# A gated mix of an S5 scan and an H3 long convolution: ssm_D put into the kernel's first column by ScalarE, and two orders of TensorE's work changed

## The chip, the cores and the metric

The kernel runs on one core of a Trainium2 chip. The metric is the time of one execution on the device, in microseconds (us), lower being better. The time before is 382.72 us, the median of three runs (378.66, 382.72 and 385.46). A further execution was profiled. In the text TensorE is PE (PEld its weight loads), VectorE DVE, ScalarE ACT, GpSimd POOL and SyncE SP, as in the profile.

## What is computed

Two layers over the same x (2048 x 1024, bf16) are mixed by a gate for each row. One is a diagonal state-space layer with complex states (S5); the other, H3, shifts k with a kernel of four taps, multiplies by v, convolves every channel causally with a kernel as long as the sequence, adds the input times ssm_D, and multiplies by q, which here is x.

```python
g = sigmoid((x * gate_w).sum(-1, keepdims=True))
Bu = einsum("bld,pd->blp", x, B_bar)            # B_bar complex
h[t] = Lam_bar * h[t - 1] + Bu[t]
a = 2 * einsum("blp,dp->bld", h, Cmat).real + x * Dskip
k_shift = sum over t of k_pad[:, t:t + S] * shift_k[:, ks - 1 - t]
kv = k_shift * v
y = irfft(rfft(kv, 2 * S) * rfft(ssm_k, 2 * S))[:S]
y = y + kv * ssm_D
b = x * y
out = g * a + (1 - g) * b
```

Adding kv * ssm_D after a convolution is the same as adding ssm_D to the first tap of the convolution's kernel, ssm_k[:, 0]. Both kernels do it in that way.

## The kernel before, in words

**Stages.** The 1024 channels of H3 are done in eight groups of 128, numbered 0 to 7; loop c of `for c in range(NC - 1)` (line 1190) works on several groups at once, as a software pipeline: the products of group c, the spectra of group n = c + 1, the folds and taps of group nn = c + 2, and the inverse of group c - 1. Beside them TensorE does the first S5 products ("B's half tiles": tiles `odd` and `even` of Bu, the generator `parts`, line 1187). After the loops come the rest of S5: products with B (tile `both`), scans on VectorE, products with C (tile `psy`), the mix and the stores.

**One group of H3.** The sequence is cut into four blocks of 512, and a transform of the block is computed by matmuls with tables of cosines and sines (CF, SF, NCF forward; CI, SI back). Ahead of the forward transform a block is folded into its even and odd parts about the middle.

- `fold_columns` (line 506) folds ssm_k's group (tile kn, channels on partitions) for groups 0 and 2 to 6. Its first step writes the reversed first half `lo` (`back`), on ScalarE for all groups but 0. Its second and third step each fill one PSUM tile `foldk` by eight matmuls against the identity, four from kn and four from lo, and ScalarE copies it into `eok`, half mt = 0 and half mt = 1. In the tile mt = 1, two more matmuls with one row of weights (`withD`, lines 522 to 526) add ssm_D, read from the row sD (sD is the first partition of `rows_`). Groups 1 and 7 are folded by `fold_K` and `mirror_K`, which add ssm_D by a matmul too.
- `fwd_K(n, fis)` (line 636) makes K's spectrum, one PSUM tile `psk` for each of four values of fi, eight matmuls each (four for group 7). The first matmul of a tile reads half 0 of eok, the second half 1. ScalarE copies psk into one of two buffers, in the trace BT.
- `taps` and `times_v` (lines 573 and 603) make k_shift * v; `times_v` has a product on VectorE, then two matmuls into `mirror`, which ScalarE copies as `lo`, then VectorE's `ev`, and a gather, an adding DMA issued by POOL, ks<-lo.
- `fwd_V` (line 674) makes v's spectrum (`psv`), from ev and ks; ScalarE copies it into Vh.
- `products` (line 687) multiplies the spectra on VectorE, ending with two writes to Vh.
- `inverse` (line 769) reads Vh by 16 matmuls into two tiles `psz`; ScalarE copies each into cv, and SP stores it to cv_scr in DRAM.

**What sets the order.** Every engine's instructions are written in a fixed order: `put` (line 93) chains each to the one before on its engine, so the order of the calls in the loop is the order on each engine. Each step waits on its engine until its operands are there. All PSUM tiles come from one pool of four (line 82): a tile takes the place of the fourth before it and waits until that one is copied out. The pool for eok has one buffer, that for lo two. DMAs are issued by SP in the order of the calls; an issue that waits holds up all behind it. `hold` (line 182) has ScalarE write one column of a tile, so that a load into it waits for ScalarE.

**The loop around the change (lines 1233 to 1322), from c = 1.** The order is: the inverse of c - 1, the mirror of times_v, four steps of products, the rest of times_v, the matrices of taps (`dgs`), the first step of fold_columns, `fwd_K` for fi 0 and 1, then 2 and 3, the rest of fold_columns, half tiles, taps, loads, the rest of products, `fwd_V` for fi 0 and 1, half tiles, `fwd_V` for fi 2 and 3. In loop 0 (lines 1192 to 1226) the rest of fold_columns(2) follows fwd_V (`run(fk)`, line 1216) and is TensorE's last work in that loop. In loop 5 the last two half tiles follow `fwd_V(6)`.

Of the kernel before, what the change touches and what calls it, by code (L numbers as in the profile page):

```python
# [10 lines left out]
ACT = mybir.ActivationFunctionType  # L11
BF16 = mybir.dt.bfloat16
F32 = mybir.dt.float32
# [7 lines left out]
def kernel(  # L21
# [76 lines left out]
    def mm(o, l, r, first, last):  # L98
        put("pe", nc.tensor.matmul, o, lhsT=l, rhs=r, start=first, stop=last)
# [15 lines left out]
    def copy(o, a):  # L115
        put("dve", V.tensor_copy, o, a)

    def act(o, i, **kw):
        put("act", nc.scalar.activation, out=o, in_=i, **kw)
# [34 lines left out]
    sD = rows_[0:1]  # L154
    skr = rows_[32:32 + ND, 0:128 * KS].rearrange("j (p k) -> j p k", k=KS)
    gwr = rows_[32:32 + ND, 128 * KS:128 * KS + 128]
    prow = rows_[64:64 + 3 * ND, 0:128]

    nc.scalar.dma_start(out=skr, in_=B_shift_k.rearrange("(j p) k -> j p k", p=128))
# [159 lines left out]
    copy(fr_, fr_i)  # L319
    pcol = consts.tile([128, 3 + KS, ND], F32, name="pcol")  # L320
    gwb = consts.tile([128, ND], BF16, name="gwb")
    pcol2 = consts.tile([128, 4, ND], F32, name="pcol2")
    ident2 = consts.tile([128, 64], BF16, name="ident2")
    psp = ps2([128, 2, 512], "p")
# [12 lines left out]
    def columns():  # L337
        mm(psp[:, 0, 0:3 * ND], prow, ident[64:64 + 3 * ND, 64:64 + 3 * ND], True, True)
        copy(pcol[:, 0:3], psp[:, 0, 0:3 * ND].rearrange("p (i j) -> p i j", j=ND))
        yield  # L340
        psp2 = ps2([128, 2, 512], "p")
        mm(psp2[:, 1, KS * ND:(KS + 1) * ND], gwr, ident[32:32 + ND, 32:32 + ND], True, True)
        for q in range(4):
            for t in range(2):
                mm(psp2[t * 64:t * 64 + 64, 1, 64 + q * ND:64 + (q + 1) * ND],
                   skr[:, q // 2 * 64:q // 2 * 64 + 64, q % 2 + 2 * t], ident[32:32 + ND, 32:32 + ND], True, True)
        yield
        copy(gwb, psp2[:, 1, KS * ND:(KS + 1) * ND])
        copy(pcol2, psp2[:, 1, 64:64 + 4 * ND].rearrange("p (i j) -> p i j", j=ND))
        tt(ident2, ident[:, 0:64], ident[:, 64:128], ALU.add)  # L350

# [154 lines left out]
    def fold_columns(c):  # L506

        kn = lds.pop(("kn", c)).rearrange("p (a t) -> p a t", t=TB)
        back = eo_pool.tile([128, 4, 2, 128], BF16, name="lo", bufs=2)
        rev = back.rearrange("p a f d -> p a (f d)"), kn[:, :, 255::-1]  # L510
        if c == 0:
            copy(*rev)
        else:
            act(*rev, func=ACT.Copy)
        yield
        eo = eos["k", c] = eo_pool.tile([128, 2, 2, 4, 128], BF16, name="eok")
        for mt in range(2):
            ps = ps2([128, 4, 2, 128], "foldk")
            for a in range(4):
                mm(ps[:, a], kn[:, a, 256 + mt * 128:384 + mt * 128], idents[:, 0:2], a % 2 == 0, False)  # L520
            for a in range(4):
                withD = mt == 1 and a == 0
                mm(ps[:, a], back[:, a, mt], idents[:, 1:3], False, a % 2 == 1)
                for e in range(2 if withD else 0):

                    mm(ps[:, a, e], refl[0:1, e], sD[:, c * 128:(c + 1) * 128], False, False)
            act(eo[:, :, mt], ps.rearrange("p a e d -> p e a d"), func=ACT.Copy)
            yield
# [123 lines left out]
    def first_K():  # L652

        eo, KH[0] = eos["k", 0], spectrum("K", 0)
        pss = [ps2([128, 2, 4, 128], "psk") for fi in range(2)]
        for mt in range(2):
            for fi, ps in enumerate(pss):
                fsl = slice(fi * 128, (fi + 1) * 128)
                for cc in range(2):
                    mm(ps[:, cc], (CF, SF)[cc][:, mt, fsl], eo[:, cc, mt], mt == 0, False)  # L660
                    mm(ps[:, cc, 1:4], (SF, NCF)[cc][:, mt, fsl], eo[:, 1 - cc, mt, 0:3], False, mt == 1)
                if mt == 1 and fi == 0:
                    act(of_tile(KH[0], fi), ps, func=ACT.Copy)
                elif mt == 1:
                    copy(of_tile(KH[0], fi), ps)
# [455 lines left out]
    def step(gen):  # L1121
        next(gen, None)

    def run(gen):
        for _ in gen:
            pass
# [32 lines left out]
    load("kT", 1)  # L1159
    load("v", 1)  # L1160
    load("kn", 1)
    first_K()
    run(angles)
    fwd_V(0, (0, 1))
# [25 lines left out]
    for c in range(NC - 1):  # L1190
        n, nn = c + 1, c + 2
        if c == 0:
            load("kn", 2)
            load("kT", 2)
            load("v", 2)
            load_BT(0, 0)
            load_xT(0, (1,))
            p1 = products(0, 1)
            fwd_K(n, (0, 1))
            steps(p0, 2)  # L1200
            run(tv)
            dg = dgs(nn, True)
            steps(p1, 2)
            step(p0)
            step(p1)
            run(p0)
            taps(nn, dg)
            step(sp)
            fk = fold_columns(nn)
            step(fk)  # L1210
            fwd_K(n, (2, 3))
            step(p1)
            step(sp)
            fwd_V(n)
            run(p1)
            run(fk)
            tv = times_v(nn)
            step(tv)
            load("kn", 3)
            load("kT", 3)  # L1220
            load_BT(0, 1)
            apart = spread(3)
            step(apart)
            load_xT(0, (0,))
            run(apart)
            continue
        if c == 6:
            put("pool", nc.gpsimd.tensor_copy, stamp, xTs[2][:, 0, 0:HB + 1:HB])
        if c == 6:
            CT[1] = ct_pool.tile([128, 2, D], BF16, name="CT1")  # L1230
            load_CT(1)
            move(rows_, bc(A_Dskip.rearrange("(o d) -> o d", o=1), [128, D]))
        tabs, back, prod = turn_table(c - 1) if c <= NG else none, inverse(c - 1), products(c)
        step(old)
        step(tabs)
        if c == 6:
            step(parts)
        run(back)
        step(tv)
        steps(prod, 4)  # L1240
        run(tv)
        step(old)
        step(tabs)
        run(old)
        fk = none
        if nn < NC:
            dg = dgs(nn)
            if by_channel(nn):
                fk = fold_columns(nn)
                step(fk)  # L1250
        if c == 2:
            step(parts)
        fwd_K(n, (0, 1))
        if c in (2, 6):
            step(parts)
        fwd_K(n, (2, 3))
        if c == 1:
            lam_diag(0, lam_pool, True)
        if c == 4:
            step(parts)  # L1260
        if c == 6:
            run(sp)
            s5p["Q"] = s5p["wu"]
            run(turns_U[2])
            gate(0)
        step(prod)
        if nn < NC:
            if not by_channel(nn):
                fk = mirror_K(nn)
            step(fk)  # L1270
            if c < 5:
                step(fk)
            if c == 4:
                step(parts)
            if c == 1:
                load_BT(1, 0, True)
            elif c in (2, 4):
                load("v", nn, True)
            step(parts)
            taps(nn, dg)  # L1280
            if c == 5:
                load("v", nn)
                load_xT(2, held=True)
            if nn + 1 < NC:
                load("kT", nn + 1, True)
                load("kn", nn + 1)
                apart = spread(nn + 1)
                step(apart)
                if c == 1:
                    load_BT(1, 1)  # L1290
                elif c in (2, 3):
                    load_xT(1, (3 - c,))
                run(apart)
        step(prod)
        run(fk)
        run(prod)
        if n == NC - 1:
            overlap_K(n)
        if nn < NC:
            tv = times_v(nn)  # L1300
            step(tv)
            step(parts)
        else:
            run(next(tiles))
            CT[0] = ld.tile([128, 2, D], BF16, name="CTa", tag="ld")
            hold(CT[0][:, 0, 0:1])
            load_CT(0)
            load_BT(2, 0)
            load_BT(2, 1)
            run(next(tiles))  # L1310
            run(next(tiles))
        fwd_V(n, (0, 1))
        if c < 6 and c != 4:
            step(parts)
            if c in (1, 3):
                step(parts)
        fwd_V(n, (2, 3))
        if c in (4, 5):
            step(parts)
        if c == 1:  # L1320
            lam_diag(1, lam_pool)
        old = tabs
# [291 lines left out]
```

## Time and profile before

| | |
|---|---|
| median of three runs | 382.72 us (378.66 to 385.46) |
| the profiled execution | 379.12 us, its span 377.3 us |
| granted TensorE clock | 1.00 |
| busy, of 377.3 us: PE, DVE, ACT, POOL | 370.3, 367.8, 303.9, 76.3 us |
| the chain that ended last: PE, issue, DMA | 90%, 5%, 3% |
| HBM read and written | 16.01 and 8.39 MB |

The profile is one execution. Its rows come from several views: the page; groups of instructions; the waits (engine, what it was about to write, whom it waited for: total us, times, longest us); the chain of waits, which goes back from the last instruction to whatever released it; windows (length, busy us of PE, PEld, DVE, ACT and POOL with the number of instructions, the granted clock, the share of the DMA engines, GB/s); and the timeline (start, length in us, engine, line, operation, written tile <- read tiles, shape, count). Nearly every instruction has line 95, that of `put`, so rows are told apart by their tiles. A row with a count groups successive instructions: its length runs from the first's start to the last's end. A matmul's row is longer than its share of the engine, because matmuls overlap: the distance between starts, the pitch, is what one costs.

### The profile page before, as it was taken

The numbers are of one execution on the slowest core, as the hardware profiler recorded it, in microseconds if no ns is written. First come the engines' busy times: TensorE is split into PE (matmuls) and PEld (weight loads), VectorE is DVE, ScalarE is ACT, GpSimd is POOL, SyncE is SP. The second block draws the span as 40 slices with busy tenths as digits, with TensorE's granted clock in tenths as the row PEclk, the third lists the DMA queues.
The fourth block names the chain that finished last, engine by engine and source line by source line (L and its number), as shares of the span: only waits on it lengthen the run. The fifth ranks groups of instructions, "written<-read, shape, count | busy, mean of one in ns | idle before, by whom it ended". The sixth has DMA issues, their size and how long they took to land.

```text
span 377.3 us, 6661 instructions
## 1 busy us (share of the span) xinstructions
PE 370.3 (98%) x2442; PEld 201.8 (53%) x2477; DVE 367.8 (97%) x596; ACT 303.9 (81%) x465; POOL 76.3 (20%) x106
## 2 busy tenths in 40 slices
PE   8999999999999999999999999999999999999996
PEld 5657567575674847644454444444444444444444
DVE  8999999999999999999999999999999999999975
ACT  5979998988979999687999699978879967946301
POOL 4011030120301203022012013122425323532000
PEclk9999999999999999999999999999999999999999
DMA  7889999999989879998999999746999998996223
GB/s 169 169 141 244 222 219 202 234 217 223 222 188 214 166 167 197 195 202 145 222 210 236 225 197 241 165 75 117 193 240 159 270 247 180 193 248 119 57 83 112
DMA packets 121827, 70.99 MB, mean 188 GB/s; under 512 B 98425, under 2 KB 103425, under 8 KB 121794
## 3 DMA queue, kind: packets, MB, share of 16 engines
q1 hardware_dynamic: 108416, 45.90, 54.6%
q0 software_dynamic: 12256, 24.38, 37.4%
q10 hardware_dynamic: 1122, 0.28, 0.4%
q8 instruction: 19, 0.31, 0.3%
q14 instruction: 14, 0.11, 0.1%
HBM read 16.01 MB, written 8.39 MB: 65 GB/s over the span
## 4 chain that ended last, share of the span: by engine, by line
PE 90%; issue 5%; DMA 3%; SPq 0%; POOL 0%; ACT 0%; DVE 0%; POOLq 0%; ACTq 0%
PE psy L95 29%; PE both L95 22%; PE psk L95 11%; PE psz L95 6%; PE psv L95 6%; PE taps L95 4%; PE foldk L95 4%; PE even L95 3%; PE odd L95 3%; DMA ks<-lo 2%; DMA kT<-in_B_k_dram 1%; PE p L95 1%; PE mirror L95 1%; SPq L95 0%; POOL acc L95 0%
## 5 line engine op out<-in xcount | busy, mean ns | idle before, releaser
L95 PE MATMUL psy<-CT,U 128*128 128x512 bf16 (+1 forms) x418 | 92.7, 374 | 0.4
L95 PEld LDWEIGHTS <-U 128*128 128x128 bf16 x492 | 48.1, 98 | 55.6 <-issue 0.3
L95 PEld LDWEIGHTS <-BT 128*128 128x128 bf16 x544 | 50.5, 98 | 33.5 <-issue 0.2
L95 DVE TENSOR_TENSOR wkh<-BT,Vh 128x2048 bf16<-128x2048 bf16 (+3 forms) x31 | 44.6, 1458 | 0.0
L95 POOL DMA_DIRECT2D U<-Q x26 | 26.6, 1035 | 80.6 <-ACT Q L95 33.0
L95 DVE TENSOR_TENSOR acc<-BT,Vh 128x4096 bf16<-128x4096 bf16 (+3 forms) x19 | 36.9, 1948 | 0.3 <-ACT Vh L95 0.2
L95 ACT ACTIVATE Q<-U,lam 128x512 bf16<-128x512 bf16 (+1 forms) x60 | 35.0, 626 | 1.4 <-issue 1.3
L95 PE MATMUL both<-xT,BT 128*128 128x512 bf16 x157 | 35.2, 379 | 0.2
L95 ACT ACTIVATE Vh<-psv 128x1024 bf16<-128x1024 f32 x32 | 30.6, 1033 | 5.6 <-PE psv L95 5.5
L95 DVE TENSOR_TENSOR_SCAN A<-rv,init,A 128x256 bf16<-128x256 f32 x48 | 34.4, 736 | 0.0
L95 DVE TENSOR_TENSOR acc<-acc,wkh 128x1024 bf16<-128x1024 bf16 (+4 forms) x30 | 32.7, 1128 | 0.1
L95 ACT ACTIVATE BT<-psk 128x1024 bf16<-128x1024 f32 x31 | 30.1, 1046 | 2.3 <-PE psk L95 2.2
L95 ACT ACTIVATE U<-both 128x512 bf16<-128x512 f32 x44 | 24.3, 594 | 8.1 <-PE both L95 7.8
L95 POOL DMA_DIRECT2D acc<-wkh x8 | 9.7, 1218 | 100.7 <-DVE wkh L95 100.7
L95 PEld LDWEIGHTS <-SF 128*128 128x128 bf16 x184 | 18.0, 98 | 19.6 <-issue 0.9
L95 PE MATMUL psk<-eok,SF 128*128 128x384 bf16 (+1 forms) x118 | 28.0, 354 | 0.2
L95 ACT ACTIVATE BT<-psy,gcols 128x1024 bf16<-128x1024 f32 (+1 forms) x6 | 6.3, 1043 | 25.6 <-issue 14.6
L95 PE MATMUL psz<-Vh,CI 128*128 128x512 bf16 x64 | 24.3, 379 | 0.0
L95 PE MATMUL psz<-Vh,SI 128*128 128x512 bf16 x64 | 24.3, 379 | 0.0
L95 PEld LDWEIGHTS <-kT 128*128 128x128 bf16 x352 | 21.5, 101 | 1.6 <-DMA kT<-in_B_k_dram 1.1
L95 PE MATMUL taps<-dg,kT 128*128 128x128 bf16 (+1 forms) x352 | 22.1, 212 | 0.1
L95 DVE TENSOR_TENSOR U<-U,trn 128x512 bf16<-128x512 bf16 (+1 forms) x60 | 22.0, 390 | 0.1
(225 smaller groups left out, 780.1 us busy)
## 6 DMA issues: line engine op xcount, KB each, us to landing
U<-Q POOLq DMA_DIRECT2D x26, 256.0 KB, 4.7
acc<-wkh POOLq DMA_DIRECT2D x6, 768.0 KB, 8.1
cv_scr<-cv SPq DMA_DIRECT2D x16, 256.0 KB, 3.6
kn<-in_B_ssm_k_dram SPq DMA_DIRECT2D x6, 512.0 KB, 3.9
v<-in_B_v_dram SPq DMA_DIRECT2D x2, 1024.0 KB, 6.9
out_dram<-m SPq DMA_DIRECT2D x8, 256.0 KB, 4.2
BT<-cv_scr SPq DMA_DIRECT2D x7, 256.0 KB, 6.0
out_dram<-BT SPq DMA_DIRECT2D x7, 256.0 KB, 2.0
```

The source lines that it names most:

```text
L95: i = f(*a, **kw)
```

## The change

Three things are changed.

1. ssm_D for groups 2 to 6. ssm_D is loaded a second time, as eight rows of 128 (drow, a part of `rows_`), by an issue on SP behind the loads of group 1. One matmul against the identity turns it into columns, and ScalarE copies them to `dcol`. In fold_columns ScalarE then adds a group's column to kn's first column, in place, ahead of the reversing copy; the matmuls of `withD` remain for group 0 alone.
2. K's spectrum. From loop 1 on, `fwd_K` for fi 0 and 1 stands in front of the inverse; fi 2 and 3 stay where they were. In loop 6 all four stand in front.
3. B's half tiles. At the end of loop 5 all that is left of `parts` runs in front of `fwd_V(6)`, v's sixth spectrum.

```diff
@@ -154,6 +154,7 @@
     gwr = rows_[32:32 + ND, 128 * KS:128 * KS + 128]
+    drow = rows_[32:32 + ND, 128 * KS + 128:128 * KS + 256]
@@ -319,6 +320,7 @@
     gwb = consts.tile([128, ND], BF16, name="gwb")
+    dcol = consts.tile([128, ND], F32, name="dcol")
@@ -340,12 +342,14 @@
         mm(psp2[:, 1, KS * ND:(KS + 1) * ND], gwr, ident[32:32 + ND, 32:32 + ND], True, True)
+        mm(psp2[:, 1, (KS + 1) * ND:(KS + 2) * ND], drow, ident[32:32 + ND, 32:32 + ND], True, True)
...
         copy(gwb, psp2[:, 1, KS * ND:(KS + 1) * ND])
+        act(dcol, psp2[:, 1, (KS + 1) * ND:(KS + 2) * ND], func=ACT.Copy)
@@ -506,6 +510,8 @@
         kn = lds.pop(("kn", c)).rearrange("p (a t) -> p a t", t=TB)
+        if c > 0:
+            act(kn[:, 0, 0:1], kn[:, 0, 0:1], func=ACT.Identity, bias=dcol[:, c:c + 1])
@@ -519,7 +525,7 @@
-                withD = mt == 1 and a == 0
+                withD = c == 0 and mt == 1 and a == 0
@@ -1159,6 +1165,7 @@
     load("kn", 1)
+    move(drow, B_ssm_D.rearrange("(j p) -> j p", p=128))
     first_K()
@@ -1235,6 +1242,7 @@
         if c == 6:
             step(parts)
+        fwd_K(n, (0, 1) if c < 6 else range(NFI))
         run(back)
         step(tv)
@@ -1250,10 +1258,10 @@
         if c == 2:
             step(parts)
-        fwd_K(n, (0, 1))
         if c in (2, 6):
             step(parts)
-        fwd_K(n, (2, 3))
+        if c < 6:
+            fwd_K(n, (2, 3))
@@ -1300,6 +1308,8 @@
             tv = times_v(nn)
             step(tv)
             step(parts)
+            if c == 5:
+                run(parts)
```

## The prediction

> **What bounds the kernel now.** I read the head of the page first, then the same busy times cut into stretches, then the list of waits.
>
> ```profile
> PE 370.3 (98%) x2442; PEld 201.8 (53%) x2477; DVE 367.8 (97%) x596; ACT 303.9 (81%) x465; POOL 76.3 (20%) x106
> ...
> 43.33:66.51 23.18, 23.07 (x200) 15.13 (x202) 23.15 (x20) 21.94 (x38) 3.11 (x4) 1.00 1.13 205
> ...
> 89.95:113.30 23.35, 23.24 (x199) 14.97 (x200) 23.32 (x20) 21.18 (x34) 3.10 (x4) 1.00 0.96 211
> ...
> 185.15:377.30 192.15, 188.22 (x958) 88.42 (x974) 185.47 (x381) 141.66 (x221) 49.02 (x57) 1.00 0.87 179
> ...
> PE psv L95 <- DMA ks<-lo: 0.8, 1, 0.8
> ...
> PEld L95 <- DVE Vh L95: 0.6, 2, 0.4
> ```
>
> TensorE works 370.3 of 377.3 us and VectorE 367.8. The stretches run from one inverse to the next in loops c = 1 and c = 3, and from the last loop to the end (columns: length, busy us of PE, PEld, DVE, ACT, POOL with counts, clock, DMA). TensorE and VectorE fill a loop to 0.1 us; ScalarE leaves 1.2 to 2.2. So a microsecond that TensorE loses or gains in the loops is one at the end, unless VectorE holds it there. Its last scan rows say that it does not:
>
> ```profile
> 358.62 0.49 DVE L95 TENSOR_TENSOR U<-U,trn 128x256 bf16<-128x256 bf16 x2
> ...
> 358.57 12.03 PE L95 MATMUL psy<-CT,U 128*128 128x512 bf16 x54
> ```
>
> Half of the last result is there by 359.1; of the 54 matmuls from 358.57 (pitch 0.22) the last 28, which read it, start near 364.6. VectorE could be 5 us later, or TensorE 5 us earlier, before one waits for the other there.
>
> So TensorE binds, and the change aims at two of its waits: 0.8 us for v's sixth spectrum on the gather ks<-lo, and 0.6 us in which the weight loads waited for VectorE's Vh.
>
> **The change, part by part.**
>
> (1) ssm_D by ScalarE. In loops 0 to 4 (fold_columns of channels 2 to 6) TensorE loses two one-row matmuls each time:
>
> ```profile
> 42.63 0.28 PE L95 MATMUL foldk<-rows,refl 1*128 1x128 bf16 x2
> 42.84 0.50 PE L95 MATMUL foldk<-ident,lo 128*128 128x256 bf16 x3
> 43.34 0.39 PE L95 MATMUL psz<-Vh,CI 128*128 128x512 bf16 x1
> ```
>
> They hold TensorE from 42.63 to 42.84: 0.21 us, five times 1.05. Behind them three matmuls of pitch 0.11 end their slots at 43.17, and the inverse starts at 43.34: here the wait for Vh costs TensorE 0.17 us. That, and not 0.6, is what a spectrum in front of the inverse can fill.
>
> ```profile
> 20.14 0.51 PE L95 MATMUL p<-ident,rows 8*128 8x8 bf16 x9
> ...
> 12.78 3.80 SPq L95 DMA_TRANSPOSE kn<-in_B_ssm_k_dram  x1
> ...
> 18.00:19.00 1.00, 1.00 (x22) 1.00 (x20) 1.00 (x2) 1.00 (x2) 0.00 (x0) 1.00 0.10 19
> ...
> 107.00 0.21 ACT L95 ACTIVATE kT<-pih 128x1 bf16<-128x1 f32 x1
> ```
>
> The added matmul (drow) is one more in a group of nine: 0.06. Its load is queued on SP behind kn's transposes and issues near 16.6; between 18 and 19 the DMA engines are down to a share of 0.10, and TensorE wants the row at 20.2, 3.6 us after the issue. I take 0; the other end is 2 us, for TensorE and for VectorE's copy of the same tile. SP's next load waits for room in any case.
>
> ScalarE gains five one-column additions and dcol. The nearest row is the one-column hold, 0.21; since the reversing copy behind reads the result I take 0.25, ends 0.1 and 0.4. The Trainium skill, "ScalarE: Activation LUTs", Rules for kernel authors, budgets about 0.3 us for an ACTIVATE with a bias operand; by it the five would come to 1.5 instead of 1.25 us, and the sum would be 0.05 larger. No row here shows a bias from a column of this width.
>
> (2) K's spectrum first: loop 1. In loop 0 fold_columns(2) is TensorE's last work, so the tile eok that fwd_K(2) reads has only just been folded, and ScalarE copies it out last in a run without gaps:
>
> ```profile
> 36.93 1.04 ACT L95 ACTIVATE lo<-kn 128x1024 bf16<-128x1024 bf16 x1
> ...
> 43.30 1.98 ACT L95 ACTIVATE eok<-foldk 128x1024 bf16<-128x1024 f32 x2
> ...
> 48.52 1.09 ACT L95 ACTIVATE lo<-mirror 128x1024 bf16<-128x1024 f32 x1
> ...
> 50.38 1.11 ACT L95 ACTIVATE lo<-kn 128x1024 bf16<-128x1024 bf16 x1
> 51.32 3.83 ACT L95 ACTIVATE BT<-psk 128x1024 bf16<-128x1024 f32 x4
> 54.94 0.79 ACT L95 ACTIVATE lamd<-ident,lam 128x128 bf16<-128x128 bf16 x2
> ...
> 53.21 0.68 DVE L95 TENSOR_TENSOR ev<-ks,lo 128x1024 bf16<-128x1024 bf16 x1
> ```
>
> The inverse reads none of it and covered the copy. Now the spectrum's first matmul needs the copy's first half, the second its second half, at 45.28 + 0.25 = 45.5. Without the wait the first would start at 43.34 - 0.17 - 0.21 = 42.96 and the second at 43.18: TensorE stands 2.35 us.
>
> ```profile
> 72.14 3.03 PE psk L95 x16
> ...
> 53.45 2.06 PE foldk L95 x18
> 55.51 1.75 PE odd L95 x16
> 57.26 1.87 PE taps L95 x64
> ...
> 100.10 2.19 PE foldk L95 x18
> ```
>
> Sixteen such matmuls take 3.03, so the inverse starts at 45.5 + 2.8 = 48.3, the mirror ends near 52.3, the second half of the spectrum near 55.3. ScalarE copies behind: two spectra, cv, then lo at 53.0 to 53.9, so that VectorE's ev (53.21) is 0.7 late. From the end of lo to the end of the reversed column it took 51.5 - 49.6 = 1.9; with the addition 2.15: 56.05. The fold comes to its reversed half at 55.7: 0.35 lost. Then two spectra (0.95 each, to 57.95), six lamd (54.94 to 56.7 before, 1.9), and the fold's two copies, at 60.8 and 61.75. PSUM has four tiles: the second tile of the taps takes the place of the fold's first, and is due at 55.65 + 1.7 + 1.75 + 0.9 = 60.0: 0.8 lost. Together 1.15; ends 0 (ScalarE catches up a microsecond) and 2.
>
> (3) The other loops. The reversed column comes two spectra and an addition later, 2.15 us, and the fold comes when it did:
>
> ```profile
> 74.43 1.05 ACT L95 ACTIVATE lo<-kn 128x1024 bf16<-128x1024 bf16 x1
> ...
> 78.91 0.60 PE L95 MATMUL foldk<-ident,lo 128*128 128x256 bf16 x4
> ...
> 97.98 1.09 ACT L95 ACTIVATE lo<-kn 128x1024 bf16<-128x1024 bf16 x1
> ```
>
> Loop 2 has 3.4 us of slack (75.5 to 78.9), since a half tile of B lies ahead of the fold; loop 4 has such a tile too. Loop 3 has none: 99.07 against 100.53 (the row of 100.10 and four matmuls of 0.11), 1.46, so 0.7 lost; ends 0 and 1.5. Where ev comes late by the same two spectra, VectorE's 5 us at the end pay. The moved cv stores are two issues on SP some 2 us later:
>
> ```profile
> 118.58 1.23 SPq L95 DMA_DIRECT2D cv_scr<-cv  x2
> 128.39 0.38 SPq L95 DMA_DIRECT2D v<-in_B_v_dram  x1
> ```
>
> SP's next entry is 8 us behind. POOL's gather ks<-lo waits for ev and moves only with it, as does hr behind it.
>
> (4) v's sixth spectrum, behind the half tiles:
>
> ```profile
> 151.85 0.38 PE L95 MATMUL psv<-ev,CF 128*128 128x512 bf16 x1
> 153.07 0.59 PE L95 MATMUL psv<-ks,SF 128*128 128x512 bf16 x2 [0.84 <-DMA ks<-lo]
> ...
> 133.47 3.77 ACT L95 ACTIVATE Vh<-psv 128x1024 bf16<-128x1024 f32 x4 [0.27 <-PE psv L95]
> ...
> 153.70 3.77 ACT L95 ACTIVATE Vh<-psv 128x1024 bf16<-128x1024 f32 x4 [1.05 <-PE psv L95]
> ...
> 137.48 2.28 DVE L95 TENSOR_TENSOR acc<-BT,Vh 128x4096 bf16<-128x4096 bf16 x1
> ...
> 160.84 2.28 DVE L95 TENSOR_TENSOR acc<-BT,Vh 128x4096 bf16<-128x4096 bf16 x1
> ...
> 163.47 3.62 PE psk L95 x16
> ```
>
> One pitch after 151.85 is 152.07; the second matmul started at 153.07: 1.0 us, now filled by two half tiles of 1.75 each. Their price: Vh is copied out 2.5 us later, by 160.0 instead of 157.5; VectorE asks at 160.84, so nothing is lost, with a cover of 0.8. In loop 6 the whole spectrum of K (3.62) precedes the inverse and makes lo, and so VectorE, at most that much later: again within the 5 us.
>
> **Sum.** Gains 1.05 + 0.17 + 1.0 = 2.2. Losses 0.06 + 2.35 + 1.15 + 0.7 = 4.25. Net +2.0: span 379.3. The profiled execution took 379.12, so 381.1 by its own time. The runs shown are 378.66, 382.72 (the median) and 385.46: it stands 3.6 below the median. The mean of the four is 381.5; I predict 381.5 + 2.0 = 383.5 us.
>
> **Rivals.**
>
> *The waits are bought back* (B). If only the 2.35 remain, the sum is +0.2; if even that wait shrinks to nothing, -2.2: 379.3 to 381.7 us. For it: ScalarE's 1.2 to 2.2 us of idle in a loop. Against: the rows above show none of it between 36.9 and the fold's copy in loop 1.
>
> *The lag spreads* (C), the slower side. VectorE asks for Vh as little as 0.24 us after ScalarE has copied it (133.47 + 3.77 against 137.48), so a late TensorE makes VectorE late, and a late lo makes both. Price: the reversed column's 2.15 us unabsorbed in each of loops 1 to 4, 8.6, with the 2.35 and less 2.2: +8.75, 390.3. It decides where ScalarE falls another 1.3 us behind TensorE, the rest of loop 2's slack. Against: a late TensorE also comes late to the fold.
>
> *drow late* (D): up to 2 us at 20: 385.5.
>
> *The clock falls* (E). Every quoted stretch has a granted clock of 1.00, and TensorE's longest gap in them is 1.0 us; 2.35 is not in this trace. If the clock halved for the spectrum and inverse behind the gap (2.8 + 3.45), they would cost 6.3 more: 389.8. The Trainium skill, "TensorE: Matmul & The Clock Gate", What's actually happening, has the clock halve after an idle window of about 3.4 us; by that rule a gap of 2.35 us leaves it alone, and E does not happen.
>
> **How the numbers follow.** Forecast 0.52, B 0.25, C 0.15, D 0.05, E 0.03. "Same" means within 2% (7.6 us), about what a measurement of this kernel can tell. Faster, below 375.1, asks for more than all gains here; only the scatter of the runs could give it: 0.03. Slower, above 390.4, comes from half of C and a part of D and E: 0.10. Same: 0.87. The range takes in B but for its quickest end and leaves out most of C and E: 378.5 to 388.5.
>
> **What would show it.** Right: TensorE stands some 2.3 us near 43 to 45.5, at the second psk matmul, behind ScalarE's copy of eok; shorter waits at the second taps tile of loop 1 and at loop 3's fold; no wait on ks<-lo near 152; no foldk<-rows matmuls in the folds of channels 2 to 6; idle of 0.5 to 1.5 us on VectorE at ev or at the first product of loops 1 to 3, where it had none. Wrong: if the wait on eok stays under 1 us, if waits at taps and folds in loops 2 to 4 together exceed 2 us, or if TensorE stands at 20 us for drow.

## The result, and the profile after

The changed kernel took 381.99 us (median of 22 runs, 381.09 to 388.6), the kernel before 379.05 (22 runs, 378.15 to 385.46): a ratio of 1.0071, 95% interval 1.0051 to 1.0092, or 2.7 us more (1.9 to 3.5). That is slower by less than 2%. Ratios, here and below, leave out the runs that lie more than 1.5% above the fastest of their kernel. The profiled execution took 382.54 us, its span is 380.8 against 377.3: 3.5 us more.

Three views of the changed kernel follow: the head of the page; the stretches from the inverse in loop 1 to that in loop 2, from loop 3 to loop 4, and from the last loop's inverse to the last matmul; and TensorE's waits (us in total, times, longest).

```profile
PE 370.1 (97%) x2468; PEld 200.8 (53%) x2468; DVE 368.5 (97%) x596; ACT 305.7 (80%) x471; POOL 78.3 (21%) x106
```

```profile
48.67:72.34 23.67, 23.02 (x200) 14.94 (x198) 23.16 (x25) 20.96 (x36) 3.10 (x4) 1.00 0.94 206
95.46:119.27 23.81, 22.86 (x200) 14.88 (x198) 23.03 (x20) 21.47 (x36) 3.10 (x4) 1.00 0.99 201
186.83:377.30 190.47, 189.49 (x977) 88.44 (x975) 186.19 (x383) 141.93 (x222) 50.60 (x57) 1.00 0.93 182
```

```profile
PE psk L95 <- ACT eok L95: 2.3, 2, 1.7
PE foldk L95 <- ACT lo L95: 1.3, 2, 0.9
PE psy L95 <- ACT U L95: 1.0, 1, 1.0
```

TensorE is as busy as before (370.1 us); the span grew by idle time. In the stretch of loop 3 it works 22.86 of 23.81 us, where 0.1 us was idle before. The wait for ks<-lo (0.8) and that of the weight loads for Vh are gone from the list; the waits of psk, foldk and psy are new. The granted clock stays at 1.00.

These are the places in the changed kernel's timeline:

```profile
44.96 0.38 PE L95 MATMUL psk<-eok,CF 128*128 128x512 bf16 x1 [1.72 <-ACT eok L95]
45.87 0.38 PE L95 MATMUL psk<-eok,CF 128*128 128x512 bf16 x1 [0.54 <-ACT eok L95]
...
56.54 0.61 PE L95 MATMUL foldk<-ident,lo 128*128 128x256 bf16 x4 [0.35 <-ACT lo L95]
61.01 0.22 PE L95 MATMUL taps<-dg,kT 128*128 128x64 bf16 x2 [0.30 <-ACT eok L95]
...
81.45 0.60 PE L95 MATMUL foldk<-ident,kn 128*128 128x256 bf16 x4
83.19 1.91 PE L95 MATMUL odd<-xT,BT 128*128 128x256 bf16 x16
...
103.93 0.61 PE L95 MATMUL foldk<-ident,lo 128*128 128x256 bf16 x4 [0.95 <-ACT lo L95]
...
232.80 1.15 ACT L95 ACTIVATE Q<-CT,mc2i 128x1024 bf16<-128x1024 bf16 x1 [1.70 <-DMA U<-Q]
238.47 1.15 ACT L95 ACTIVATE pbb<-pbb,omg 128x1024 bf16<-128x1024 bf16 x1 [1.23 <-DMA pbb<-cv_scr]
...
251.82 1.02 PE L95 MATMUL psy<-CTa,U 128*128 128x512 bf16 x4 [0.97 <-ACT U L95]
```

Before, the same fold of loop 2 ran

```profile
78.47 0.60 PE L95 MATMUL foldk<-ident,kn 128*128 128x256 bf16 x4
80.53 1.91 PE L95 MATMUL odd<-xT,BT 128*128 128x256 bf16 x16
```

that is 2.06 us from its first matmul to the next tile; without the one-row matmuls it takes 1.74 (81.45 to 83.19).

Starts can be set against each other. The rows are the first matmul of the second half of channel 0's spectrum, the head of loop 2, and the gates behind loop 6's inverse, first of the kernel before, then of the changed one:

```profile
20.59 0.39 PE L95 MATMUL psk<-eok,CF 128*128 128x512 bf16 x1
66.35 0.38 PE L95 MATMUL psz<-Vh,CI 128*128 128x512 bf16 x1
166.92 0.94 PE L95 MATMUL p<-gwb,xT 128*128 128x1 bf16 x32
```

```profile
20.80 0.60 PE L95 MATMUL psk<-eok,CF 128*128 128x512 bf16 x2
69.33 0.59 PE L95 MATMUL psk<-eok,CF 128*128 128x512 bf16 x2
168.77 0.94 PE L95 MATMUL p<-gwb,xT 128*128 128x1 bf16 x32
```

I count from the first of them, since the transfer of the first kT lands up to 1.6 us apart from one execution to the next. Behind that point TensorE of the changed kernel is late by 2.77 us at the head of loop 2, 2.40 at loop 3, 2.91 at loop 4, 2.42 at loop 5, and 1.64 at the gates. It stays 1.64 until the first psy, where it becomes 2.77; from there to the last matmul both take 125.48 us. The rest of the 3.5 us is 0.21 at the start and 0.5 behind the last matmul.

### The profile page after: what moved, and what is told of

Its sections match the earlier page's. It is cut to its first block, busy times and chain, and to the rows that moved or that the text cites. A ratio compares the mean times of both kernels' runs of the same rounds, so it can differ in the third digit from the quotient of the medians.

```text
span 380.8 us, 6687 instructions
## 1 busy us (share of the span) xinstructions
PE 370.1 (97%) x2468; PEld 200.8 (53%) x2468; DVE 368.5 (97%) x596; ACT 305.7 (80%) x471; POOL 78.3 (21%) x106
## 4 chain that ended last, share of the span: by engine, by line
PE 76%; ACT 15%; SPq 3%; DMA 3%; issue 2%; DVE 0%; ACTq 0%
PE psy L95 29%; PE both L95 13%; PE psk L95 8%; PE psz L95 6%; PE psv L95 5%; PE even L95 4%; PE taps L95 4%; PE odd L95 3%; SPq L95 3%; ACT Vh L95 2%; ACT BT L95 2%; PE foldk L95 2%; ACT m L95 2%; DMA pbb<-cv_scr 1%; DMA kT<-in_B_k_dram 1%
## 5 line engine op out<-in xcount | busy, mean ns | idle before, releaser
L95 PEld LDWEIGHTS <-kT 128*128 128x128 bf16 x352 | 20.7, 98 | 3.0 <-DMA kT<-in_B_k_dram 2.1
```

Source lines behind the costliest of these rows:

```text
L95: i = f(*a, **kw)
```

## The experiments

The runs are compared with the kernel before on the same chip; the profile of a kernel is one execution. The table holds every kernel but one, which follows in the text (dcol by VectorE in the whole change). Its columns, in us: TensorE's lateness against before at the gates behind loop 6, counted from the first spectrum (before, 166.92 - 20.59 = 146.33); what is added from there to the first psy (before 81.92); the time from the end of the last matmul to the end of the span; the ratio of the runs with its interval.

| kernel | loops | to psy | last matmul to end | ratio |
|---|---|---|---|---|
| before | 0 | 0 | 2.98 | 1 |
| the change | +1.64 | +1.13 | 3.50 | 1.0071 (1.0051 to 1.0092) |
| change, loop 1 as before | -0.64 | +0.65 | 3.45 | 1.0027 (0.9999 to 1.0054) |
| only loop 1's spectrum moved | +1.33 | 0 | 3.05 | 1.0056 (1.0031 to 1.0080) |
| only ssm_D by ScalarE | +1.08 | +0.99 | 3.46 | 1.0021 (1.0000 to 1.0042) |
| only the half tiles moved | -0.79 | 0 | 2.97 | 0.9983 (0.9954 to 1.0012) |
| ssm_D, half tiles, dcol by VectorE | -0.60 | 0 | 3.47 | 1.0006 (0.9986 to 1.0026) |
| change, loops 1 and 3 as before, dcol by VectorE | -1.09 | 0 | 3.50 | 1.0035 (1.0009 to 1.0061) |
| change, fold earlier in loop 0 | +0.73 | 0 | 3.44 | 1.0043 (1.0018 to 1.0067) |
| only drow's load | -0.22 | 0 | 3.47 | 1.0022 (0.9996 to 1.0048) |
| ssm_D by GpSimd, half tiles | +10.47 | 0 | 3.46 | 1.0291 (1.0266 to 1.0317) |
| half tiles, spectrum moved in loops 2, 4, 5, 6 | -0.95 | 0 | 3.02 | 1.0010 (0.9975 to 1.0045) |
| ssm_D by VectorE, half tiles | -0.41 | 0 | 3.44 | 1.0012 (0.9988 to 1.0035) |

My theory was that the loss is loop 1: TensorE stands on eok, and ScalarE's order behind it delays that loop's fold and taps. The rival was a lag that spreads over all loops.

**Loop 1 put back, everything else as changed.**

```
-        fwd_K(n, (0, 1) if c < 6 else range(NFI))
+        if c > 1:
+            fwd_K(n, (0, 1) if c < 6 else range(NFI))
         run(back)
...
+        if c == 1:
+            fwd_K(n, (0, 1))
         if c < 6:
             fwd_K(n, (2, 3))
```

> The whole change but for loop 1, where K's spectrum goes back behind the inverse. Theory 1 (the loss is loop 1: TensorE stands on ScalarE's copy eok, and ScalarE's order behind it delays that loop's fold and taps): the wait psk on eok is gone, the taps wait of loop 1 too; gains of 1.05 (D), 0.17 (Vh) and 0.78 (ks<-lo) stay, the fold of loop 3 still loses 0.9: -1.1 us against before, with the first psy as before; if the 1.1 us that the changed kernel lost at its first psy (ScalarE's U late, behind DMA) come from the moved half tiles and loads, they recur and the sum is 0.0. Rival (the loss is spread over the loops by ScalarE's later lo): it stays above +1.5 us.

In the loops TensorE gains 2.28 us on the changed kernel (+1.64 to -0.64): the loss in the loops is loop 1's order. The runs keep +1.0 us. In the profile 0.65 of it stands in one more late transfer (a matmul that writes `both` waits 0.49 for BT) and 0.47 behind the last matmul.

**Loop 1's spectrum alone moved.**

```
+        if c == 1:
+            fwd_K(n, (0, 1))
         run(back)
...
-        fwd_K(n, (0, 1))
+        if c > 1:
+            fwd_K(n, (0, 1))
```

> The kernel before with nothing but loop 1's half spectrum of K moved in front of the inverse. Theory 1: TensorE stands 2.3 us at psk on eok, less the 0.17 that it waited for Vh and the 0.2 by which its fold ends later; the reversed column comes two spectra later, so fold and taps of loop 1 lose 0.7 together: +2.7 us. Rival (the additions of ssm_D on ScalarE carry the loss, the move alone is covered): +0.5 us at most.

TensorE waits 1.6 us for eok and is 2.12 late at loop 2. At loop 5 the wait for ks<-lo is gone, because TensorE comes later to it: 0.78 comes back without any half tile being moved. The runs show +2.1 us: one moved spectrum makes most of the change's loss. The rival falls.

**ssm_D by ScalarE alone** (the change without its three edits of order).

> The kernel before with ssm_D added by ScalarE and nothing else. Theory 1: five pairs of one-row matmuls gone from TensorE, 0.21 us each, one matmul of 0.06 added, the additions of 0.3 us hidden on ScalarE: -1.0 us. VectorE's wait of 0.5 us behind dcol at 21 us is lost again only where TensorE waits for VectorE (Vh in loop 1): then -0.5. Rival (the additions cost TensorE its folds, 0.3 us in each loop without slack): 0 to +0.5 us.

A miss: +0.8 us (0.0 to 1.6), where I expected a gain. Two rows of VectorE and one of TensorE in its profile:

```profile
21.80 0.19 DVE L95 COPY pcol<-p 128x32 f32<-128x32 f32 x1 [0.49 <-ACT dcol L95]
...
42.16 0.69 DVE L95 TENSOR_TENSOR acc<-acc,t 128x1024 bf16<-128x1024 bf16 x1 [1.04 <-DMA acc<-wkh]
...
45.49 0.39 PE L95 MATMUL psz<-Vh,CI 128*128 128x512 bf16 x1 [2.00 <-DVE Vh L95]
```

VectorE's copy pcol2 stands 0.49 us for ScalarE's dcol, which reads the same PSUM tile; the adding DMA acc<-wkh landed 1.04 us late for it as well, and TensorE stands 2.00 us for Vh at loop 1's inverse. VectorE's work of loop 0 is what sets Vh, and nothing covers it there.

Two other profiles tell the two causes apart. The change with loop 1 put back has the same order up to this point and the same 0.49, but no late DMA; the kernel with dcol by VectorE and the spectra as before (below) has neither. Their waits at the same inverse, in this order:

```profile
45.12 0.39 PE L95 MATMUL psz<-Vh,CI 128*128 128x512 bf16 x1 [0.86 <-DVE Vh L95]
```

```profile
43.45 0.39 PE L95 MATMUL psz<-Vh,CI 128*128 128x512 bf16 x1 [0.38 <-DVE Vh L95]
```

So dcol's part of the 2.00 is 0.48. Some 1.1 come with the late DMA, which the same order of work had in one profile and not in the other; without it the +1.08 in the loops would be about nothing.

The Trainium skill, "PSUM — Partial Sum Buffer", PSUM bank collisions raise a hardware error, says that the compiler's scheduler adds a dependency between two engines' accesses to one bank and quadrant, reads among themselves too. The trace agrees that such a wait is there: with both copies on VectorE it is gone.

**The half tiles alone.**

```
             step(parts)
+            if c == 5:
+                run(parts)
```

> The kernel before with nothing but the half tiles of B in front of v's sixth spectrum. Theory 1: no wait of TensorE for ks<-lo near 152, -0.8 us, and the first psy as before. Rival 1 (Vh of channel 6 comes 2.5 us later, and VectorE's products in loop 6 with it): 0 to +1. Rival 2 (the half tiles' U and the SP loads behind the stamp move, and that is what the changed kernel lost at the first psy): a wait of about 1 us of psy for ScalarE's U near 250, sum +0.3.

As expected: no wait for ks<-lo, -0.79 us up to the end, nothing at the first psy. The runs (-0.6 us, interval -1.7 to +0.5) can't tell it from before.

**dcol by VectorE, spectra as before** (ssm_D by ScalarE and the half tiles stay).

```
-        act(dcol, psp2[:, 1, (KS + 1) * ND:(KS + 2) * ND], func=ACT.Copy)
+        copy(dcol, psp2[:, 1, (KS + 1) * ND:(KS + 2) * ND])
```

> ssm_D by ScalarE and the half tiles of B in front of v's sixth spectrum, K's spectra where they were before, and dcol copied by VectorE. Theory 1 (what ssm_D alone lost came from VectorE's 0.5 us wait for ScalarE's dcol, which ends at loop 1's inverse as TensorE's wait for Vh): that wait of 0.9 to 2.0 us falls to 0.3 at most, the one-row matmuls give 1.0 and the half tiles 0.8: TensorE is 1.6 us earlier than before at loop 6, and if the 0.5 us longer last store of the kernels with ssm_D's load stays, -1.1 us in all. Rival 1 (the additions themselves or the load of drow cost it): TensorE no earlier than with ssm_D alone, +0.3 us. Rival 2 (the stage from 217 to 251 us loses its microsecond whenever drow is loaded): -0.2 us.

The wait for Vh in loop 1 falls to 0.38 (0.3 at most was expected), but TensorE is only 0.60 earlier, not 1.6. Its timeline shows three new waits (58.52 is loop 1, 100.52 loop 3, 123.77 loop 4):

```profile
58.52 0.22 PE L95 MATMUL taps<-dg,kT 128*128 128x64 bf16 x2 [0.53 <-ACT eok L95]
...
98.15 0.32 ACT L95 ACTIVATE kn<-kn,dcol 128x1 bf16<-128x1 bf16 x1
99.47 3.75 ACT L95 ACTIVATE BT<-psk 128x1024 bf16<-128x1024 f32 x4
...
100.52 0.60 PE L95 MATMUL foldk<-ident,kn 128*128 128x256 bf16 x4 [0.25 <-ACT BT L95]
...
123.77 1.91 PE L95 MATMUL even<-xT,BT 128*128 128x256 bf16 x16 [0.26 <-ACT BT L95]
```

The addition stands 0.3 us in front of the copies of psk and eok, and TensorE waits for the tiles that they free. In the old order that takes back what the one-row matmuls gave. It takes back dcol's gain too: at the head of loop 2 this kernel is 0.46 us late, and the change with loop 1 put back, which has dcol on ScalarE, 0.47.

**Only loops 1 and 3 put back** (dcol by VectorE; the spectrum stays in front in loops 2, 4, 5 and 6).

> The whole change but for loops 1 and 3, where K's spectrum goes back behind the inverse, and dcol copied by VectorE. Theory 1 (moving the spectrum costs only in loops 1 and 3; where a half tile of B lies ahead of the fold it is free): equal to the kernel with ssm_D, half tiles and no moved spectrum to 0.3 us, -1.1 us against before. Rival (ScalarE's later lo makes VectorE, and with it the last stage, late in any loop): at least 1 us slower than that kernel.

By the profile the rival falls: -1.09 in the loops, 0.49 better than without any moved spectrum, and a span of 376.7 us, shorter than before's 377.3. But the runs are at +1.3 us (0.3 to 2.3). Two of its eleven runs, 383.07 and 383.51 us, show a mean granted clock of 0.995 and 0.996, which none of the 32 runs of the kernel before that the ratio uses does; the other nine stand 0.4 us above before in the mean. The profile shows no step that costs even that; it stays open (below).

**The fold earlier in loop 0** (the whole change with one more edit of order).

```
-            fwd_V(n)
-            run(p1)
+            fwd_V(n, (0, 1))
             run(fk)
+            fwd_V(n, (2, 3))
+            run(p1)
```

> The whole change, and in loop 0 the fold of channel 2 ahead of the second half of v's spectrum, so that ScalarE copies eok two copies earlier with the same work in all. Theory 1 (the wait of 2.3 us is one of order): the waits of psk for eok fall to about 0.5 us, TensorE gains 1.8 us on the changed kernel, +0.9 to +1.2 us against before. Rival (ScalarE is simply 2.3 us behind TensorE at 43 us): TensorE waits as long, now for a PSUM tile or for Vh, and the time is that of the changed kernel, +2.9 us.

```profile
44.16 0.38 PE L95 MATMUL psk<-eok,CF 128*128 128x512 bf16 x1 [0.54 <-ACT eok L95]
54.83 0.61 PE L95 MATMUL foldk<-ident,lo 128*128 128x256 bf16 x4 [0.35 <-ACT lo L95]
```

The wait for eok falls from 2.3 to 0.54 us and the lateness at loop 2 from 2.77 to 0.94, by 1.83. The wait is one of order: ScalarE's work is the same. The fold's wait of 0.35 stays. The runs show +1.6 us (0.7 to 2.5), above the +0.9 to +1.2 that was expected, which lies inside the interval.

**drow's load alone.**

```
+    move(drow, B_ssm_D.rearrange("(j p) -> j p", p=128))
     first_K()
```

> The kernel before with the load of drow added on SP, and nothing that reads it. Theory 1 (the load is hidden in the loops): 0.0 us up to the last matmul; if the last store ends 0.5 us later as in the three profiles with this load, +0.5 us. Rival (one more transfer on SP shifts the late loads, and with them the U<-Q and pbb waits of ScalarE between 217 and 251 us): a wait at the first psy of 0.8 to 1.0 us as well, +1.5 us.

Nothing is lost up to the last matmul (-0.22 us), and the span ends 0.5 us later behind it. Below are the last instruction of VectorE and two windows behind it, up to the end of the span, for this kernel (span 379.1), and then for the kernel before (377.3):

```profile
375.67 0.48 DVE L95 SCALAR_TENSOR_TENSOR BT<-psy,gcols,xlast 128x256 bf16<-128x256 f32 x1 [0.67 <-PE psy L95]
...
376.15:377.40 1.25, 0.00 (x0) 0.00 (x0) 0.00 (x1) 0.00 (x0) 0.00 (x0) 1.00 0.22 65
377.40:379.10 1.70, 0.00 (x0) 0.00 (x0) 0.00 (x0) 0.00 (x0) 0.00 (x0) 1.00 0.00 0
```

```profile
374.35 0.48 DVE L95 SCALAR_TENSOR_TENSOR BT<-psy,gcols,xlast 128x256 bf16<-128x256 f32 x1 [0.68 <-PE psy L95]
...
374.83:376.08 1.25, 0.00 (x0) 0.00 (x0) 0.01 (x1) 0.00 (x0) 0.00 (x0) 1.00 0.22 66
376.08:377.30 1.22, 0.00 (x0) 0.00 (x0) 0.00 (x0) 0.00 (x0) 0.00 (x0) 1.00 0.00 0
```

From that instruction's end to the end of the span it is 2.95 us here and 2.47 before. The store itself takes no longer, though the expectations speak of a later last store: in both kernels the DMA engines (share 0.22) are done within 1.25 us. Behind that the span goes on for 1.70 us here and 1.22 before, and in that time the profile shows no instruction and no transfer. In the table all nine kernels that load drow stand at 3.44 to 3.50, the four that don't at 2.97 to 3.05, and in each of them the transfers end within the same 1.25 us.

**dcol by VectorE in the whole change.**

> The whole change with dcol copied by VectorE instead of ScalarE. Theory 1 (in loop 1 TensorE stands on eok longer than VectorE is late, so dcol's wait costs the changed kernel nothing there): VectorE's 0.5 us wait is gone, TensorE's waits for eok stay at 2.3, and up to the last loop it loses 1.6 us on before, as with the change itself; the last store ends 0.5 us later. If ScalarE's waits for U<-Q and pbb between 217 and 251 us stay below 2 us in all, there is no wait at the first psy and the sum is +2.1; if they come again at 2.9, +3.1. Rival (VectorE's lateness was part of the loss): +1.5 us or less without such waits.

Ratio 1.0101 (1.0052 to 1.0149), +3.8 us, or +3.1 by the medians: no better than the change. In its profiled execution TensorE's second psk matmul of loop 1 starts 25.07 us behind the first spectrum (48.16 - 23.09), as in the changed kernel (45.87 - 20.80): the wait for eok hides VectorE's lateness, so dcol costs nothing there, and the rival falls.

Behind that matmul the granted clock (the last column but two) falls in this execution:

```profile
48.16 0.38 PE L95 MATMUL psk<-eok,CF 128*128 128x512 bf16 x1 [0.54 <-ACT eok L95]
...
45.53:48.55 3.02, 0.77 (x5) 0.29 (x4) 3.02 (x4) 3.02 (x5) 0.00 (x0) 1.00 1.21 145
48.55:51.95 3.40, 3.18 (x10) 1.45 (x10) 3.40 (x3) 2.16 (x4) 0.00 (x0) 0.50 1.14 213
```

TensorE worked 0.77 of 3.02 us, with the same two gaps of 1.72 and 0.54 us as in the changed kernel, and then ran for 3.40 us at half the clock; the inverse starts 1.68 us later than there (52.65 - 23.09 against 48.68 - 20.80). The clock falls once more behind a wait of 2.48 us near 250. This is the prediction's rival E, and the rule by which a gap of 2.35 us leaves the clock alone does not hold in this execution; where a rule and the trace differ, the trace decides. The changed kernel's profiled execution, with the same gaps, kept 1.00, so such a gap brings the fall in some executions and not in others. From here on the execution is not compared.

**ssm_D by GpSimd** (spectra as before, half tiles, dcol by VectorE, drow loaded on ScalarE's queue).

```
+            put("pool", nc.gpsimd.tensor_tensor, out=k0, in0=k0, in1=dcol[:, c:c + 1], op=ALU.add)
...
+        add_D(nn)
         tabs, back, prod = turn_table(c - 1) if c <= NG else none, inverse(c - 1), products(c)
```

> K's spectra where they were before, half tiles of B in front of v's sixth spectrum, and ssm_D added by GpSimd at the head of each loop instead of by ScalarE; dcol copied by VectorE; drow loaded on ScalarE's queue at the start instead of on SP. Theory 1 (the additions on ScalarE delay its copies of psk and eok, and TensorE pays 0.3 to 0.5 us for them in loops 1, 3 and 4): those three waits are gone, the one-row matmuls give 0.8 us (the fifth is taken by the wait for Vh), the half tiles 0.8: TensorE 1.5 us earlier than before at loop 6; the last store as before if the extra transfer on SP is what lengthens it: -1.5 us in all, or -1.0 with the longer store. Rival (GpSimd's addition is late behind its gathers, and the reversed column with it): a wait of foldk or taps of 0.5 us or more in loops 1 to 4, and -0.5 us at most.

A miss in another way, +11.0 us. Loop 2, on GpSimd, VectorE, ScalarE and TensorE:

```profile
70.94 14.50 POOL L95 TENSOR_TENSOR kn<-kn,dcol 128x1 bf16<-128x1 bf16 x1 [14.50 <-DMA kn<-in_B_ssm_k_dram]
...
84.17 1.22 DVE L95 TENSOR_TENSOR acc<-acc,wkh 128x2048 bf16<-128x2048 bf16 x1
91.97 1.29 DVE L95 TENSOR_TENSOR acc<-acc,wkh 128x1024 bf16<-128x1024 bf16 x2 [6.58 <-DMA acc<-wkh]
...
85.47 1.06 ACT L95 ACTIVATE lo<-kn 128x1024 bf16<-128x1024 bf16 x1 [10.88 <-POOL kn L95]
...
87.49 1.01 PE L95 MATMUL psk<-eok,CF 128*128 128x512 bf16 x2 [10.27 <-ACT BT L95]
```

The one-column addition took 14.5 us (the one before it 0.19 us). VectorE worked without a gap from before it until 85.39, and the addition ended at 85.44. (VectorE's next instruction needed the DMA acc<-wkh, which POOL issues behind the addition; that is why it stopped.) Of the other four additions, of 0.19 to 2.78 us, three end within 0.1 us of a gap of VectorE too; the one in loop 3 took 1.32 us and ended between two instructions of VectorE that left none. Behind the long one the reversed column came 10.9 us late and TensorE stood 10.3. The Trainium skill, "SBUF — State Buffer", SBUF: two separate sides, says that VectorE and GpSimd share a pair of ports as an exclusive lock, held for a whole instruction; the row fits that GpSimd was shut out, and shows it across some 12 instructions of VectorE rather than one.

The granted clock fell here as well:

```profile
87.49:91.40 3.91, 3.69 (x12) 1.83 (x13) 0.00 (x0) 2.99 (x4) 0.92 (x2) 0.50 1.05 184
```

Half of the 3.69 us that TensorE was busy there, some 1.8 us, would not be there at the full clock (an estimate from this row); it is part of the +11.0. With the load on ScalarE's queue the span still ends late (3.46), so it isn't SP's queue that does it.

**Half tiles, and the spectrum in front in loops 2, 4, 5 and 6, ssm_D as before.**

> The kernel before with K's spectrum in front of the inverse in loops 2, 4, 5 and 6 and the half tiles of B in front of v's sixth spectrum; ssm_D by TensorE as before. Theory 1 (in loops with a half tile of B ahead of the fold, or no fold by columns, the order of spectrum and inverse costs and gives nothing): TensorE as with the half tiles alone, -0.8 us. Rival (the later lo makes VectorE and the last stage late): a wait of 0.3 us or more for Vh, U or CT behind loop 4, 0 to +1 us.

-0.95 against -0.79 with the half tiles alone: where a half tile of B lies ahead of the fold, or no fold by columns follows, the move costs nothing and gives 0.16. The runs (+0.4 us, -0.9 to +1.7) show no gain.

**ssm_D by VectorE** (spectra as before, half tiles).

```
-        steps(prod, 4)
+        steps(prod, 2)
+        add_D(nn)
+        steps(prod, 2)
```

> K's spectra where they were before, half tiles of B in front of v's sixth spectrum, dcol copied by VectorE, and ssm_D added to the column by VectorE between two products at the head of each loop, 0.1 us each, so that neither ScalarE nor GpSimd has any of it. Theory 1 (0.3 us on ScalarE in front of its copies is what TensorE pays for in loops 1, 3 and 4): the waits that ssm_D on ScalarE brought there (taps on eok 0.5 in loop 1, about 0.35 each in loops 3 and 4, for psk's tile) are gone and the one-row matmuls show as a gain: TensorE 1.5 us earlier than before at loop 6, against 0.6 with ScalarE's additions; the last store 0.5 us longer as with every kernel that loads drow: -1.0 us. Rival 1 (those waits come from the fold being 0.2 us shorter, not from the additions): they stay, 0.6 us earlier and -0.1 in all. Rival 2 (VectorE stands for kn's load behind a product): a wait of VectorE on kn, and of TensorE on Vh, 0 to +2 us.

TensorE's waits, and the addition in the view of the tile kn (times, and ns min, median, max):

```profile
PE psz L95 <- DVE Vh L95: 1.1, 3, 0.5
PE psz L95 <- ACT Vh L95: 0.4, 1, 0.4
```

```profile
L95 DVE TENSOR_TENSOR kn<-kn,dcol x5: 153/153/164, 29.3 to 119.0; 128x1 bf16<-128x1 bf16 x5
```

The waits in loops 1, 3 and 4 on ScalarE's copies are gone, as the theory said; but TensorE now waits 1.1 us for VectorE's Vh and 0.4 more for a Vh put down to ScalarE, and is only 0.41 earlier. VectorE is as full as TensorE: what TensorE saves in a loop it waits for at the next inverse.

No kernel here is shown to beat the one before. Against the changed kernel several do, the half tiles alone most clearly: the intervals 0.9954 to 1.0012 and 1.0051 to 1.0092 don't meet.

## Why the prediction was right, and where it was not

In the loops the net was forecast at +2.0 and is +1.64. Term by term, by starts of TensorE:

- *eok, 2.35*: the second psk matmul starts at 45.87. The fold that began at 41.32 and takes 1.74 ends at 43.06, one pitch of 0.22 later is 43.28: 2.59. Right, in place and size.
- *Loop 1's fold and taps, 0.35 and 0.8*: the fold takes 2.28 (55.59 to 57.87) instead of 1.74, the taps 2.33 (59.61 to 61.94) instead of 1.86: 0.54 and 0.47, together 1.0 for 1.15. Right.
- *Loop 3's fold, 0.7*: it takes 2.87 (102.38 to 105.25): 1.13. Larger, within the ends of 0 and 1.5.
- *The one-row matmuls, 0.21 each*: 0.32 each (2.06 to 1.74), so 1.6 for 1.05. The quoted starts left out what they cost the matmul ahead of them, which in the fold of loop 0 starts 0.20 us before them (42.63 in the prediction's rows), where the pitch is 0.11:

```profile
42.43 0.27 PE L95 MATMUL foldk<-ident,lo 128*128 128x256 bf16 x1
```

- *The additions on ScalarE, 0.25 each*: 0.28 to 0.34. (The prediction says that 0.3 each would add 0.05 to its sum; by its own working the folds of loops 1 and 3 would each lose 0.05 more, so 0.1.)
- *Half tiles, 1.0*: 0.79 by the kernel with nothing else.

Not seen was that the spectrum itself gets faster when it is split by the inverse, where its four tiles had waited on ScalarE. In loop 3 before,

```profile
93.72 0.59 PE L95 MATMUL psk<-eok,CF 128*128 128x512 bf16 x2
...
100.03 0.60 PE L95 MATMUL foldk<-ident,kn 128*128 128x256 bf16 x4
```

the four tiles took 6.31 us; two of them take 3.02 after (99.36 to 102.38), so 0.27 was idle; in loop 4 it was 0.15.

The sum of these, with 0.06 for drow's matmul and 0.16 for the wait for Vh (0.17 forecast): 2.59 + 1.0 + 1.13 + 0.06 less 1.6, 0.16, 0.79 and 0.42 is 1.8, against 1.64 measured. That the net came within 0.4 us of the forecast is in part luck: single terms were off by 0.2 to 0.6 us, in both directions.

The lag did not spread: loops 2 and 4 gave back 0.37 and 0.49. The waits of VectorE at Vh (0.24, 0.38, 0.75 in loops 2 to 4) and ev (0.23 in loop 1) came where they were looked for, three of them below the 0.5 to 1.5 us forecast, and drow was in time.

Rival E, the falling clock, did not occur in the changed kernel's profiled execution: the clock stayed at 1.00 behind gaps of 1.72 and 0.54 us. It was not ruled out, though. The kernel with dcol by VectorE had it behind the same gaps, at a price of 1.7 us and not 6.3, since the clock was low for 3.4 us only. Over 380 us such a stretch lowers the mean clock to 0.9955 (an estimate, 1 - 0.5 x 3.4 / 380). Four of the changed kernel's 22 runs have a mean of 0.995 or 0.996; they take 383.5 us in the mean, the other 17 that the ratio uses 382.0. So 0.3 of the 2.7 us goes with a lower clock. Where it fell in those runs is not known, and the wait for eok can't be its only source: the half tiles alone, which don't have that wait, show a mean of 0.996 or less in 4 of 12 runs, the kernel before on the chips of the experiments in 5 of 105.

Two steps failed, both outside the loops. The first is "VectorE could be 5 us later, or TensorE 5 us earlier, before one waits for the other there", taken to stand for the whole stage behind loop 6. The stage from 217 to 251 us is tight too, on ScalarE: there it waits for transfers (U<-Q, pbb<-cv_scr). Where its waits add up to 2.93 us (the change) or 2.89 (ssm_D alone), TensorE stands 0.97 or 0.83 at the first psy. (For ssm_D alone the list names VectorE's CT, which was done at 246.7; but in both profiles psy starts 1.13 us after ScalarE begins its last four copies of U, 250.69 to 251.82 and 250.23 to 251.36, against 245.71 and 248.84 before.) Where they are 0.97 to 1.70 (five kernels) or nothing, it doesn't stand at all. So about 2 us are free, by the two profiles that exceed them, and what exceeds them is paid. The second is drow's load, priced at 0: hidden in the loops, but the span then ends 0.5 us later, behind the last transfer.

Why those transfers are late in some executions is not settled. The kernels that share the moved order had the psy wait or did not, and for the kernel with loops 1 and 3 put back the profile is shorter than before's while the runs are 1.3 us longer (0.4 without the two at a lower clock). Of the 2.7 us, 1.64 and 0.5 make 2.1; of the remaining 0.6, 0.3 goes with the lower clock of four runs, and the rest would fit a wait of 1.13 in some of the runs. This last part is argued, not shown.

The gain of ssm_D was wrong as a separate term: in the order of before it is a loss or nothing (+0.8 us alone, 0.0 to 1.6). In the changed kernel the folds are shorter by it; I read this as real there because two spectra stand between the fold and the inverse and cover VectorE's Vh and ScalarE's additions, which no run tests alone.

The forecast of 383.5 stood on a mean of 381.5 from four runs, and 22 runs have a median of 379.05: the level was 2.4 us too high, the difference 0.7 too low (+2.0 forecast, +2.7 measured, 1.9 to 3.5). That 383.5 lies only 1.5 us from 381.99 comes from these opposite errors, and that is luck. Of the difference, only the part in the loops is what the prediction had worked out.

## What to carry to other kernels

Before work is moved in front of a stage, ask which copy it reads and where that copy stands in the copying engine's order: here the inverse had covered 2.6 us of ScalarE, and one edit that copies the tile earlier took 1.8 of it back. Where two engines are both 97% busy, as here, a saving on one was only worth what the other had in hand at the next handover, so test each part of a change alone: in the profiles one gained (0.79), one lost (1.33 for loop 1's spectrum), and ssm_D gained nothing. An instruction of one column is not free on a full engine: 0.3 us on ScalarE in front of the copies that release PSUM tiles cost TensorE 0.25 to 0.53 us in three of five loops.

## What the hardware showed that I had not expected

A one-column addition on GpSimd can last as long as VectorE runs without a gap: 0.19 us in one loop, 14.5 us in the next. Two gaps of TensorE of 1.72 and 0.54 us, 0.4 us of work between them, left the granted clock at 1.00 in one execution and brought it to 0.50 for 3.4 us in another. And one more small load in the first 20 us, on either of two queues and read or not, goes with a span that ends 0.5 us later, 1.7 instead of 1.2 us behind the last transfer, in nine kernels of nine; the cause stays open.
